# Other rank offsets for the last four batches of an attention and mixer kernel

## The chip, the cores and the metric

The kernel runs on one core of a Trainium2 chip. The metric is the device time of one execution in microseconds; the median of three runs is given. Beside it stands one profiled execution, whose trace the text reads.

## The reference

There are 8 batches of 576 positions, 8 heads of 64. First comes causal attention in a window of 128 positions with a bias that falls with distance, then a mixer: one MLP over the positions (token mixing) and one over the channels, each with a residual.

```python
def attention(q, k, v):                       # (8, 8, 576, 64)
    scores = q @ k.T / 8 + slopes * -abs(rel)  # masked to 0 <= rel < 128
    return softmax(scores) @ v
def mixer(x):                                 # (8, 576, 512)
    h = relu(x.T @ w_tok1) @ w_tok2            # 576 -> 256 -> 576
    u = x + h.T
    return u + relu(u @ w_ch1) @ w_ch2         # 512 -> 1536 -> 512
```

## The kernel before

The kernel works in bf16 with f32 sums. Positions are cut into blocks of 128; two batches make a pair, whose two remainders of 64 positions share one block, TAIL. For each batch `b` there are two strands of work.

`side(b)` is attention and token mixing. For each block the transposed `q` and `k` come from a DMA transpose on SyncE's queue (line 621, into `qkT`). Scores are matmuls of 64 rows (line 672) into both pairs of PSUM banks; ScalarE takes the exponential (695), VectorE masks (705), TensorE multiplies by `v` (739), VectorE normalises into `xb` (752, 755). `token_mix` then multiplies by the token weights (784, 794, ReLU at 802/803, 827, 823 for TAIL), adds the residual into `ub` (845), and SyncE's queue transposes `ub` into `uT` (853).

`main(b)` is channel mixing. `chunk` multiplies `uT` by the first weights (line 1024; all blocks of `uT` must have landed) with a ReLU on ScalarE or VectorE (1030, 1031); `tail_piece` does so for TAIL (1067). The second weights use seven products on halves, as in Strassen's scheme (`second`, line 1212), on sums that VectorE makes (1049); VectorE adds each product to the output (1180), and it is stored (1192). TAIL's second product is at 1112, its sum at 1119, its stores at 1129. The last batch also does its first product in that scheme (`halves`, line 910; `unit`, 946 to 990). Its last product, `last_product`, is at 1241: it adds to a bank after the eviction of product 7, its sums are at 1245 and its two stores at 1248, one from SyncE's queue and one from ScalarE's.

`main(b)` and `side(b+1)` are laid over each other. The order is not written by hand: every step is registered with `plan.op` (engine, estimated cost, rank), and `Plan.run` walks through time with these estimates. Of the steps that an engine could start soonest it takes the one of lowest rank. Ranks within a strand rise by the steps' costs (656 for half a product of 1212, 648 for three matmuls of 1112, 864 for a chunk); `side(b+1)` is squeezed into the first 38% of the ranks of `main(b)`. GpSimd's DMA issues keep the order in which they were registered. Then each step's rank is shifted by a random offset:

```python
        dice = [random.Random(x) for x in SEEDS]
        for o in ops:
            if SEEDS[o.part]:
                o.rank += dice[o.part].uniform(-SHIFT, SHIFT)     # SHIFT = 1500.0
```

The part is set in the loop over the batches, `plan.part = b + 1`, ahead of `main(b)` and `side(b + 1)`. So entry 5 of `SEEDS` covers `main(4)` and `side(5)`, entry 6 `main(5)` and `side(6)`, entry 7 `main(6)` and `side(7)`, entry 8 `main(7)`. An entry of 0 means no offsets; entry 4, for `main(3)` and `side(4)`, is 0 before and after.

Idle instructions are registered last, with a rank above all others: blocks of copies of one column on ScalarE (lines 1286, 1287) and of small memsets on VectorE (1288, 1289), each block after a point of the planned time. Idle matmuls (1296) are put only into gaps of TensorE in the first 60 us of the plan.

Of the kernel before, what the change touches and what calls it, by code (L numbers as in the profile page):

```python
# [10 lines left out]
ACT = mybir.ActivationFunctionType  # L11
# [54 lines left out]
class Plan:  # L66
# [6 lines left out]
    def buf(self, name, choice=None):  # L73
        return Buf(self.rings[name], choice or self.rings[name].each)
# [43 lines left out]
    def run(self):  # L118
        ops = self.ops
# [3 lines that stand above are left out]
                o.rank += dice[o.part].uniform(-SHIFT, SHIFT)  # L123
# [210 lines left out]
RANKH = 0  # L334
RELU = 350
SUMS_AT = 60e3
SEEDS = [45795, 495947, 190309, 331881, 0, 67117, 67408, 179769, 445757]
SHIFT = 1500.0
UNIT_LATE = False
SECOND_LATE = True  # L340
# [28 lines left out]
def kernel(  # L369
# [76 lines left out]
    zero = const.tile([P, P], BF16, name="zero")  # L446
# [25 lines left out]
    pe_, act_, dve_ = nc.tensor, nc.scalar, nc.vector  # L472
# [53 lines left out]
    for i_, name in enumerate("qk"):  # L526
# [3 lines left out]
            out=buf()[:, i, :, :], in_=raw.rearrange("p (h d) -> p h d", h=H)), -100 + i_, makes=buf, after=4.8e3 + 600 * i_)  # L530
# [64 lines left out]
    for e in range(2):  # L595
        def go(e=e):
            for i in range(2):
                dve_.tensor_copy(out=maskt[:, e, :, 0, i * R : (i + 1) * R], in_=masks[:, e, :, 0, 0:R])
            dve_.tensor_copy(out=maskt[:, e, :, 1, :], in_=masks[:, e, :, 1, :])
            dve_.memset(maskt[0:R, e, :, 1, R:P], 0.0)  # L600
# [682 lines left out]
        base += n  # L1283

    for eng, n, cost, at, go in (
            ("ACT", 9, 200, 262e3, lambda: act_.copy(out=zero[:, 0:1], in_=zero[:, 2:3])),
            ("ACT", 9, 200, 262e3, lambda: act_.copy(out=zero[:, 0:1], in_=zero[:, 2:3])),
            ("DVE", 5, 60, 266.5e3, lambda: dve_.memset(zero[:, 1:2], 0.0)),
            ("DVE", 5, 60, 266.5e3, lambda: dve_.memset(zero[:, 1:2], 0.0))):
        plan.op(eng, n * cost, lambda n=n, go=go: [go() for _ in range(n)], 1e9, after=at)  # L1290
# [41 lines left out]
```

## Time and profile before

| | us |
|---|---|
| median of 3 runs | 278.81 |
| lowest, highest | 278.72, 279.33 |
| profiled execution | 278.47 |
| its span, first to last instruction | 276.7 |
| TensorE busy | 268.5 |
| VectorE busy | 209.0 |
| ScalarE busy | 139.2 |

The span leaves out 1.8 us of the execution that lie around the program's instructions. "PE" in a row is TensorE, "PEld" its weight loads, DVE VectorE, ACT ScalarE; SPq and ACTq are the queues from which SyncE and ScalarE issue transfers. `L1212` is line 1212 of the kernel. A timeline row gives start, length, engine, line, operation, output and inputs, and the number of instructions merged; in square brackets stands the engine's idle time just before, with what ended it. The length of a matmul row runs to the end of the last matmul's passage, which overlaps the start of the next row.

### The profile page before, as it was taken

Reading aid. Unit: us, or ns where it says so; the run is one execution under the profiler, and the core shown is the slowest. Engines: PE = TensorE matmul, PEld = TensorE weight load, DVE = VectorE, ACT = ScalarE, POOL = GpSimd, SP = SyncE. Lnnn points to the kernel's source line nnn. Section 1 sums busy time; section 2 is a strip of 40 time slices with the busy share of each in tenths; the row PEclk is TensorE's granted clock in tenths of the full one; section 3 lists DMA queues with packets and bytes.
Section 4 is the critical chain, followed back from the end, with each engine's and each line's share of the span. In section 5 each row is a group of like instructions: output and inputs, shape, how many; then the busy total and the mean of one; then the engine's idle time right before and its main releaser. Section 6 shows DMA issues by size and latency. Waiting matters only on the chain.

```text
span 276.7 us, 6959 instructions
## 1 busy us (share of the span) xinstructions
PE 268.5 (97%) x2789; PEld 179.6 (65%) x2825; DVE 209.0 (76%) x496; ACT 139.2 (50%) x237; POOL 115.8 (42%) x146
## 2 busy tenths in 40 slices
PE   7999999999999999999999999999999999999994
PEld 3665655775686555585567655576667645679884
DVE  7577689978897469853989478763989549886984
ACT  5572884436950298107951096206860079205660
POOL 8998965940356037900585009600472220013000
PEclk9999999999999999999999999999999999999999
DMA  9999999999899999999999979999499750043014
GB/s 132 159 141 164 182 192 189 155 124 207 138 110 111 181 243 133 124 142 181 173 136 151 206 193 100 138 144 243 65 117 97 194 147 2 2 114 135 1 50 143
DMA packets 167553, 38.45 MB, mean 139 GB/s; under 512 B 155808, under 2 KB 166688, under 8 KB 167520
## 3 DMA queue, kind: packets, MB, share of 16 engines
q0 software_dynamic: 116112, 20.03, 94.9%
q1 hardware_dynamic: 50224, 17.57, 33.6%
q10 hardware_dynamic: 1184, 0.39, 0.6%
q8 instruction: 22, 0.36, 0.6%
q14 instruction: 11, 0.09, 0.1%
HBM read 35.85 MB, written 9.44 MB: 164 GB/s over the span
## 4 chain that ended last, share of the span: by engine, by line
PE 89%; DMA 4%; DVE 2%; POOL 1%; ACT 1%; issue 1%; POOLq 0%; ACTq 0%
PE ps L1212 26%; PE ps L1024 22%; PE ps L739 6%; PE ps L672 6%; PE ps L784 5%; PE ps L827 5%; PE ps L1067 4%; PE ps L1112 4%; PE ps L946 3%; DMA WC<-in_moe_w_ch_dram 3%; PE ps L1296 2%; DMA qk<-in_q_dram 2%; PE ps L632 1%; PE ps L794 1%; POOL qk L515 1%
## 5 line engine op out<-in xcount | busy, mean ns | idle before, releaser
L1024 PE MATMUL ps<-uT,WC 128*128 128x512 bf16 x306 | 77.4, 379 | 1.3 <-DMA WC<-in_moe_w_ch_dram 0.3
L695 ACT ACTIVATE pe<-ps 128x1024 bf16<-128x1024 f32 (+1 forms) x76 | 63.4, 888 | 29.9 <-PE ps L672 29.6
L515 POOL DMA_DIRECT2D v<-in_v_dram x40 | 34.1, 866 | 93.6 <-PE ps L739 88.5
L1030 ACT ACTIVATE r<-ps 128x512 bf16<-128x512 f32 x75 | 44.4, 601 | 41.1 <-PE ps L1024 39.1
L1024 PEld LDWEIGHTS <-WC 128*128 128x128 bf16 x328 | 29.1, 98 | 30.6 <-issue 1.4
L705 DVE TENSOR_TENSOR pe<-pe,mask 128x1024 bf16<-128x1024 bf16 (+1 forms) x64 | 38.2, 609 | 8.8 <-ACT pe L695 8.3
L1212 PEld LDWEIGHTS <-r 128*128 128x128 bf16 x372 | 35.9, 98 | 7.2 <-issue 0.2
L515 POOL DMA_DIRECT2D qk<-in_k_dram x39 | 34.5, 891 | 3.0 <-DMA v<-in_v_dram 1.7
L515 POOL DMA_DIRECT2D qk<-in_q_dram x39 | 34.0, 878 | 0.7 <-DMA WC<-in_moe_w_ch_dram 0.6
L1212 PEld LDWEIGHTS <-s 128*128 128x128 bf16 x288 | 27.5, 98 | 6.0 <-issue 1.3
L755 DVE TENSOR_TENSOR xb<-ps,rt 128x256 bf16<-128x256 f32 (+1 forms) x72 | 29.1, 417 | 0.7
L739 PEld LDWEIGHTS <-pe 128*128 128x128 bf16 (+1 forms) x560 | 22.3, 98 | 9.0 <-DVE pe L705 2.6
L739 PE MATMUL ps<-v,pe 128*128 128x65 bf16 (+1 forms) x560 | 26.3, 194 | 0.4 <-DVE pe L705 0.2
L1212 PE MATMUL ps<-WC,r 128*128 128x256 bf16 x192 | 25.4, 273 | 0.0
L1212 PE MATMUL ps<-WT,s 128*128 128x256 bf16 x192 | 24.6, 273 | 0.1
L845 DVE TENSOR_TENSOR ub<-ps,xb 128x512 bf16<-128x512 f32 x34 | 21.2, 683 | 1.8 <-PE ps L827 1.8
L1212 PE MATMUL ps<-WT,r 128*128 128x256 bf16 x180 | 22.4, 273 | 0.0
L672 PEld LDWEIGHTS <-qkT 64*128 64x128 bf16 x560 | 14.8, 94 | 11.2 <-issue 9.8
L1180 DVE TENSOR_TENSOR ob<-ps,ub 128x512 f32<-128x512 f32 x21 | 14.3, 686 | 9.4 <-PE ps L1212 9.2
L672 PE MATMUL ps<-qkT 64*128 64x128 bf16 (+1 forms) x304 | 19.4, 216 | 0.4
L1072 ACT ACTIVATE r2t<-ps 128x512 bf16<-128x512 f32 x12 | 7.2, 603 | 22.7 <-PE ps L1067 22.7
L752 DVE RECIPROCAL rt<-ps 128x4 f32<-128x4 f32 (+1 forms) x76 | 12.5, 175 | 7.6 <-PE ps L739 7.0
(102 smaller groups left out, 347.8 us busy)
## 6 DMA issues: line engine op xcount, KB each, us to landing
v<-in_v_dram POOLq DMA_DIRECT2D x32, 128.0 KB, 5.0
out_dram<-ob SPq DMA_DIRECT2D x16, 256.0 KB, 2.6
qk<-in_k_dram POOLq DMA_DIRECT2D x31, 128.0 KB, 5.1
qk<-in_q_dram POOLq DMA_DIRECT2D x31, 128.0 KB, 5.0
WC<-in_moe_w_ch_dram POOLq DMA_DIRECT2D x8, 384.0 KB, 8.8
out_dram<-raw SPq DMA_DIRECT2D x7, 256.0 KB, 2.7
out_dram<-ob POOLq DMA_DIRECT2D x5, 256.0 KB, 3.6
out_dram<-raw POOLq DMA_DIRECT2D x3, 256.0 KB, 2.9
```

The lines of the kernel that those rows point to most:

```text
L515: nc.gpsimd.dma_start(out=to()[p0 : p0 + n, :, :], in_=rows(src, b, s0, n))
L672: pe_.matmul(wide(e)[:, i, kind, a:z], lhsT=ts[kb]()[e * D : (e + 1) * D, NHP + i, :], rhs=ts[blk]()[e * D : (e + 1) * D, i, a:z], start=n ...
L695: act_.activation(out=pb()[:, e, :, lo:, c0:c1_], in_=wide(e)[:, :, lo:, c0:c1_], func=ACT.Exp, scale=scale)
L705: dve_.tensor_tensor(out=o, in0=o, in1=heads(mk, es), op=ALU.mult)
L739: pe_.matmul(view()[a:z, at, i, :], lhsT=pb()[:, e, i, kind, a:z], rhs=vb()[:, h, 0 : D + 1], start=m == 0, stop=m == len(mms) - 1, skip_g ...
L755: dve_.tensor_tensor(out=x4(), in0=view()[r0:r1_, :, :, 0:D], in1=rt()[r0:r1_, 0:n, :, :].broadcast_to([r1_ - r0, n, 4, D]), op=ALU.mult)
L784: pe_.matmul(t1[j]()[:, :], lhsT=W1[:, c, j * P : (j + 1) * P], rhs=xb()[:, blk, :], start=c == 0, stop=False)
L845: plan.op("DVE", 690, lambda blk=blk, ht=ht, hs=hs: dve_.tensor_tensor(out=ub()[:, blk, :], in0=ht()[:, hs], in1=xb()[:, blk, :], op=ALU.a ...
L1024: pe_.matmul(ct()[:, :], lhsT=WC1[:, cb, t * P : (t + 1) * P], rhs=uT()[:, cb, :], start=cb == 0, stop=cb == NCB - 1)
L1030: plan.op("ACT", 600, lambda t=t, ct=ct: act_.activation(out=r2()[:, t, :], in_=ct()[:, :], func=ACT.Relu), rk, part=(r2, t), uses=[ct], o ...
L1180: dve_.tensor_tensor(out=v, in0=both(bk), in1=src, op=ALU.add)
L1212: pe_.matmul(of(bk, c), lhsT=l(t, c), rhs=w(t), start=first, stop=g == 1 and t == HK - 1, skip_group_check=True)
```

## The change

Four of the nine entries of `SEEDS` are replaced, so the steps of `main(4)` to `main(7)` and of `side(5)` to `side(7)` get other offsets; those of `main(6)` and `side(7)` get none. Each of the two blocks of idle copies on ScalarE has eleven copies where it had nine, with the estimated cost to match (2200 where it was 1800).

```diff
-SEEDS = [45795, 495947, 190309, 331881, 0, 67117, 67408, 179769, 445757]
+SEEDS = [45795, 495947, 190309, 331881, 0, 148233, 244960, 0, 319733]
...
-            ("ACT", 9, 200, 262e3, lambda: act_.copy(out=zero[:, 0:1], in_=zero[:, 2:3])),
-            ("ACT", 9, 200, 262e3, lambda: act_.copy(out=zero[:, 0:1], in_=zero[:, 2:3])),
+            ("ACT", 11, 200, 262e3, lambda: act_.copy(out=zero[:, 0:1], in_=zero[:, 2:3])),
+            ("ACT", 11, 200, 262e3, lambda: act_.copy(out=zero[:, 0:1], in_=zero[:, 2:3])),
             ("DVE", 5, 60, 266.5e3, lambda: dve_.memset(zero[:, 1:2], 0.0)),
             ("DVE", 5, 60, 266.5e3, lambda: dve_.memset(zero[:, 1:2], 0.0))):
```

## Prediction

> **What bounds the kernel now.** I read the page first, for the share of each engine and the transfers of code.
>
> ```profile
> span 276.7 us, 6959 instructions
> ...
> PE 268.5 (97%) x2789; PEld 179.6 (65%) x2825; DVE 209.0 (76%) x496; ACT 139.2 (50%) x237; POOL 115.8 (42%) x146
> ...
> q8 instruction: 22, 0.36, 0.6%
> q14 instruction: 11, 0.09, 0.1%
> ...
> PE 89%; DMA 4%; DVE 2%; POOL 1%; ACT 1%; issue 1%; POOLq 0%; ACTq 0%
> ```
>
> TensorE is busy for 97% of the span, and 89% of the chain that ended last is TensorE. Busy time alone proves little, since matmuls overlap each other, so I looked into the part that the new offsets reach, first at a window of it, then at the starts of its matmuls.
>
> ```profile
> 185.00:221.00 36.00, 35.63 (x378) 24.10 (x382) 25.30 (x56) 16.66 (x24) 11.43 (x14) 1.00 1.07 144
> ```
>
> The columns after the length are the busy time of TensorE, of its weight loads, of VectorE, ScalarE and GpSimd, then the clock, here full (1.00), and DMA. The timeline of TensorE at the start of batch 6 shows the rate:
>
> ```profile
> 215.67 0.81 PE L1112 MATMUL ps<-WC,r2t 128*128 128x512 bf16 x3
> 216.32 1.47 PE L1212 MATMUL ps<-WT,r 128*128 128x256 bf16 x12
> 217.63 1.46 PE L1112 MATMUL ps<-WC,r2t 128*128 128x512 bf16 x6
> 218.92 1.47 PE L1212 MATMUL ps<-WT,r 128*128 128x256 bf16 x12
> 220.45 0.59 PE L1112 MATMUL ps<-WC,r2t 128*128 128x512 bf16 x2
> 221.03 1.02 PE L1024 MATMUL ps<-uT,WC 128*128 128x512 bf16 x4
> 221.99 0.40 PE L672 MATMUL ps<-qkT 64*128 64x128 bf16 x8
> 222.32 1.04 PE L1024 MATMUL ps<-uT,WC 128*128 128x512 bf16 x4
> ```
>
> Take start from start. Three matmuls of 512 columns need 216.32 - 215.67 = 0.65 us, 0.217 each; twelve of 256 columns need 217.63 - 216.32 = 1.31 us, 0.109 each, so one group of six in line 1212 is worth 0.655 us. Every row starts where the row before has used up its matmuls at this rate, with one exception, the start of line 1024 at 221.03. The weight loads show it as well:
>
> ```profile
> 220.12 0.42 PEld L1112 LDWEIGHTS <-r2t 128*128 128x128 bf16 x3
> 221.00 0.56 PEld L1024 LDWEIGHTS <-WC 128*128 128x128 bf16 x4 [0.45 <-issue]
> ```
>
> Three weights were loaded for line 1112, so one matmul record is missing and there were three. The twelve of 218.92 are through at 220.23, the three of line 1112 at 220.88, and line 1024 starts at 221.03: TensorE stood still for 0.15 us. The rows of the transposes that make `uT` say why:
>
> ```profile
> L853 SPq DMA_TRANSPOSE uT<-ub x4: 1217/1229/1288, 213.5 to 217.4; - x4
> ...
> DMA to landing us min/median/max: 2.3/2.7/3.5
> ```
>
> The last of the four is issued at 217.4 and, with the longest landing of 3.5 us, is there at 220.9. Line 1024 reads all four blocks, so it can start only then. What stands between the token mixing and this point, the second products (1212) and the tail block (1112), is cover for that chain, and it was used up to the last group. So the kernel is bound by matmul work, which this change leaves as it is, and by three such handovers plus the end, where order decides whether cover suffices.
>
> **What the change touches, and what each part costs.**
>
> *The matmul work itself: 0.* Ranks decide order alone; every product stays, and the filler matmuls are placed only in the first 60 us of the plan. Order could save or add changes of shape: four matmuls of line 1024 take 221.99 - 221.03 = 0.96 us ahead of line 672 where 4 x 0.217 = 0.87 are due, and the eight of line 672, four pairs of a quarter of 0.217 each, 0.22 us, take 0.33. One excursion to 64 rows costs about 0.2 us. Each score needs both pairs of PSUM banks, so two scores don't stand side by side without waiting for ScalarE; I count the number of excursions as unchanged and keep 0.2 us to either side.
>
> *The handover to batch 5* (new offsets of part 5).
>
> ```profile
> L853 SPq DMA_TRANSPOSE uT<-ub x4: 1190/1252/2225, 176.0 to 182.1; - x4
> ...
> DMA to landing us min/median/max: 2.5/5.0/6.2
> ```
>
> ```profile
> 185.09 1.89 PE L1024 MATMUL ps<-uT,WC 128*128 128x512 bf16 x7
> 186.81 1.47 PE L1212 MATMUL ps<-WT,r 128*128 128x256 bf16 x12
> ```
>
> The last landing is at 182.1 + 2.5 = 184.6 or later, and line 1024 starts at 185.09: at most 0.5 us to spare. But twelve matmuls of line 1212 still stand behind, at 186.81, so another order has 1.31 us of cover in hand here. I cost it at 0, with 0.65 us if one group is missing.
>
> *The handover to batch 6* (part 6). Here nothing is in hand: the margin is -0.15 us and behind 221.03 come only line 1024, which waits for the same transposes, and scores. If the token mixing comes earlier by 0.15 us or one group of the second products later, 0.15 us is gained. If one group of six goes ahead of the token mixing instead, the stall grows by 0.655 us; two groups, 1.31. Offsets of up to 1500 on ranks that lie 656 apart can move a group past two of its neighbours. I take one group, +0.65 us, since the order of before has no spare here, and any other order has more ways to lose cover than to find it.
>
> *The handover to batch 7* (part 7, whose offsets are now all zero).
>
> ```profile
> L946 PE MATMUL ps<-uT,WC x5: 272/272/273, 252.0 to 252.5; 128*128 128x256 bf16 x5
> L853 SPq DMA_TRANSPOSE uT<-ub x4: 1191/1227/1259, 242.6 to 247.8; - x4
> ...
> DMA to landing us min/median/max: 2.3/2.4/3.4
> ```
>
> Landed at 247.8 plus 2.3 to 3.4, 250.1 to 251.2, and needed at 252.0: 0.8 to 1.9 us to spare, so one group may be lost without cost, and two cost at most 0.5. I take 0. SyncE's queue issues these transposes in the planned order too: one that is put behind a transpose for `qkT` (these are issued 1.2 to 1.3 us apart) lands as much later, which is again two groups.
>
> *The end* (part 8).
>
> ```profile
> 270.69 1.15 PE L1112 MATMUL ps<-WC,r2t 128*128 128x256 bf16 x9
> 270.89 0.69 DVE L1180 TENSOR_TENSOR ob<-ps,ob 128x512 f32<-128x512 f32 x1
> 271.67 1.47 PE L1241 MATMUL ps<-WT,r 128*128 128x256 bf16 x12
> 272.36 1.11 SPq L1129 DMA_DIRECT2D out_dram<-raw  x2
> 272.52 0.42 DVE L1245 TENSOR_TENSOR ob<-ps,ub 128x256 f32<-128x256 f32 x1 [0.23 <-PE ps L1241]
> ...
> 273.56 0.54 SPq L1248 DMA_DIRECT2D out_dram<-ob  x1
> 273.64 0.36 ACTq L1248 DMA_DIRECT2D out_dram<-ob  x1
> ```
>
> The last product (1241) adds to a bank that VectorE must have read after the product before: 270.89 to 271.58. Nine matmuls of the tail block, 270.69 to 271.67, fill exactly that wait. If the offsets send them ahead, TensorE idles for up to 0.98 us; three of them, 0.33. Behind the last matmul, the first half's sum is ready at 272.52 + 0.42 = 272.94, but SyncE issues two stores of the tail block until 273.47, so that store goes out at 273.56.
>
> ```profile
> out_dram<-ob SPq DMA_DIRECT2D x3, 128.0 KB, 2.3
> ...
> out_dram<-ob ACTq DMA_DIRECT2D x1, 128.0 KB, 1.8
> ```
>
> It lands at about 273.56 + 2.3 = 275.9, the other half at 273.64 + 1.8 = 275.4; an order that finishes the tail block earlier gains up to 0.4 us here, and pays with the filler. I take 0, from -0.4 to +0.98.
>
> *The four idle instructions.*
>
> ```profile
> 262.75 0.63 ACT L974 ACTIVATE r<-r 128x512 bf16<-128x512 bf16 x1 [2.03 <-DVE r L970]
> ...
> 264.18 2.00 ACT L1286 COPY zero<-zero 128x1 bf16<-128x1 bf16 x9
> 266.21 2.01 ACT L1287 COPY zero<-zero 128x1 bf16<-128x1 bf16 x9
> ```
>
> Nine take 2.00 us, eleven 11/9 of it, 2.45. Two blocks from 264.18 then end at 269.1, and ScalarE's next work is the store at 273.64: 4.6 us are left, cost 0. If a block is placed into a wait like the 2.03 us ahead of 262.75, it delays the ReLU behind it by at most 2.45 us, its whole length. Four instructions also shift where ScalarE's code is loaded. The page has 22 transfers on q8 with 0.36 MB, 16 KB each, and 11 on q14 with 0.09 MB, 8 KB each; no row shows an engine waiting for one, and I cost the shift at 0, bounded by the issue share of the chain, 1% of the span or 2.8 us, all of it over the whole run. The Trainium skill, in Runtime: NRT & Kernel Launch, section Instruction fetch mechanics, says that code comes in blocks of 16 KiB, or 256 instructions, and that crossing into the next is mostly hidden. The 16 KB transfers here agree, the 8 KB ones do not; by that rule the four cost nothing too.
>
> *The sum.* 0 for the work, 0 + 0.65 + 0 for the handovers, 0 for the end and the idle instructions: +0.65 us on the profiled execution, which took 278.47 us (its span of 276.7 and 1.8 around it): 279.1. The median of the runs, 278.81, lies 0.34 above the profiled one, so I expect **279.5 us**, 0.2% more. About 0.2%, 0.56 us, is what a measurement of this kernel can tell from no change, so this forecast lies just beyond it.
>
> **The rivals.**
>
> *Nothing is lost.* The new order covers the handover to batch 6 within a few tenths, as the old one does, and the end keeps its filler. For it: TensorE waits only 0.15 us in the row above, and the unshifted order has a place in this trace too, the handover to batch 4, where line 1024 follows without a gap:
>
> ```profile
> 154.45 1.23 SPq L853 DMA_TRANSPOSE uT<-ub  x1
> ```
>
> ```profile
> 158.30 0.40 PE L672 MATMUL ps<-qkT 64*128 64x128 bf16 x8
> 158.63 1.90 PE L1024 MATMUL ps<-uT,WC 128*128 128x512 bf16 x8
> ```
>
> There 4.2 us lie between the last issue and the use, more than a landing of 3.5. Against it: the cover at batch 6 is used up. Time: 278.3 to 279.3, most likely 278.9.
>
> *Faster.* The gain is bounded: 0.15 at batch 6, 0.4 at the stores, 0.2 for one excursion less, together 0.75 us, 278.06. Since all three are needed to pass 0.56 by much, I give it little. A wider gain would need idle time that the rows above don't leave. The Trainium skill, in Perfetto Trace Analysis, section Identifying the Most-Contended Engine, says that matmul busy time is a poor measure of headroom and that the busy share of weight loads is one to use. By that rule 65% would leave a third of the time free; the trace disagrees, since the starts of line 1212 follow at 0.109 us, the rate above, whatever the share of the loads. I give a gain beyond the bound 2 in 100.
>
> *Two places at once.* The handover to batch 6 loses two groups (1.31) and the end its filler (0.98): +2.3 us, 281.1. Or one block of idle copies falls ahead of a ReLU of the last batch, up to 2.45 us, 281.3. For it: both covers are exactly as long as what they hide. Against it: they are in different parts, with offsets of their own.
>
> *The change does nothing*, because few instructions are ready at a time and the same order comes out. Offsets that span 3000 against steps of 656 make that unlikely; its time is that of the first rival, and it is counted there.
>
> **How the numbers follow.** One group uncovered, at batch 6 or a like loss at the end (0.33 to 1.6 us, 279.1 to 280.4): 0.43, of which 0.07 stays below 0.56. Nothing lost: 0.32. Faster: 0.13, of which 0.02 stays within 0.56 and 0.02 lies beyond the bound. Two places: 0.12. So faster by over 0.2%: 0.11; within: 0.32 + 0.07 + 0.02 = 0.41; slower: 0.36 + 0.12 = 0.48. The range runs from 278.1, the bound of the gain, to 280.9, just below the sum of two places; that leaves out about 0.02 below and 0.1 above. As cases of both signs hold much of it, the likeliest one's own range is 279.1 to 280.4.
>
> **What would show it.** Right: at the start of batch 6 the weight loads of line 1024 show an idle time of 0.8 to 1.2 us instead of 0.45, and its first start follows the last landing of `uT`; batches 5 and 7 start without a gap; the two blocks of copies stand behind the last ReLU and take 2.45 us each. Wrong: line 1024 of batch 6 starts on the heels of line 1112, or the gap is at 1241, where the eviction of line 1180 would be bare, or the last store lands less than 2.3 us behind the last sum. A span that moves by more than these places add up to would mean that something outside them, code loading or the first half, has changed.

## The result and the profile after

| | before | changed |
|---|---|---|
| median, us (11 runs each) | 279.19 | 280.60 |
| lowest, highest | 278.29, 280.33 | 279.82, 281.78 |
| profiled execution | 278.47 | 280.73 |
| its span | 276.7 | 278.9 |

The ratio is 1.0054, with a 95% interval of 1.0035 to 1.0074: the change costs 0.5%, 1.5 us, the interval being 1.0 to 2.1 us. The page of the changed kernel:

```profile
span 278.9 us, 6965 instructions
...
PE 269.2 (97%) x2790; PEld 180.2 (65%) x2825; DVE 209.0 (75%) x497; ACT 139.2 (50%) x237; POOL 116.0 (42%) x146
...
q8 instruction: 22, 0.36, 0.6%
q14 instruction: 11, 0.09, 0.1%
...
PE 82%; DMA 6%; POOL 4%; DVE 4%; issue 2%; ACT 1%; DVEq 0%; POOLq 0%; ACTq 0%
```

The busy times are nearly the same. To place the 2.25 us between the two profiled spans I took three landmarks that both orders share and compared their starts: the first score of the stage in which the orders part (line 672), the first score behind the start of batch 6, and the last product (1241). TensorE's timeline of the changed kernel:

```profile
159.00 0.40 PE L672 MATMUL ps<-qkT 64*128 64x128 bf16 x8
...
219.58 1.47 PE L1212 MATMUL ps<-WT,r 128*128 128x256 bf16 x12
220.89 0.81 PE L1112 MATMUL ps<-WC,r2t 128*128 128x512 bf16 x3
221.53 1.03 PE L1024 MATMUL ps<-uT,WC 128*128 128x512 bf16 x4
222.49 0.40 PE L672 MATMUL ps<-qkT 64*128 64x128 bf16 x8
```

- Up to 159.00, where 158.30 stood before: +0.70. The order there has not changed. The other kernels with this first part reach the point between 158.4 and 159.5, so this is the spread of one execution, and no effect.
- From there to 222.49, where 221.99 stood: 0.20 less. Line 1024 starts at 221.53, right behind the three matmuls of line 1112 (220.89 + 0.65 = 221.54). The wait of 0.15 us at batch 6 is gone. But it was not the old order's: in the four other profiles of that order, taken from runs below, this stretch is 0.15 us shorter (63.54 us for 63.69; 63.49 in the changed kernel), and line 1024 follows the three matmuls of line 1112 at once, as in the run with two memsets (220.35 + 0.65 = 221.00):

```profile
220.35 0.81 PE L1112 MATMUL ps<-WC,r2t 128*128 128x512 bf16 x3
221.00 1.03 PE L1024 MATMUL ps<-uT,WC 128*128 128x512 bf16 x4
```

- From there to 1241, 272.79 for 271.67: +0.62, all of it at the start of batch 7.
- From 1241 to the end: 6.13 for 5.00 us, +1.13.

The start of batch 7, with TensorE's and VectorE's rows of the changed kernel's timeline together:

```profile
246.13 0.68 DVE L1180 TENSOR_TENSOR raw<-ps,raw 128x512 f32<-128x512 f32 x1
...
247.53 0.76 DVE L910 TENSOR_TENSOR tt<-uT 128x512 bf16<-128x512 bf16 x2 [0.73 <-DMA uT<-ub]
248.21 0.68 DVE L1180 TENSOR_TENSOR raw<-ps,raw 128x512 f32<-128x512 f32 x1
...
248.41 0.60 PE L946 MATMUL ps<-uT,WC 128*128 128x256 bf16 x4
...
248.81 0.88 DVE L910 TENSOR_TENSOR tt<-uT,tt 128x512 bf16<-128x512 bf16 x2
...
249.29 0.60 PE L946 MATMUL ps<-uT,WC 128*128 128x256 bf16 x4
249.61 0.68 DVE L1180 TENSOR_TENSOR ob<-ps,ob 128x512 f32<-128x512 f32 x1
...
250.34 1.47 PE L1212 MATMUL ps<-WT,r 128*128 128x256 bf16 x12 [0.46 <-DVE ob L1180]
```

VectorE stands for 0.73 us at line 910, the first step that needs the transposes of batch 7. Behind it in its queue stand two evictions (1180). TensorE has the transposes in time for line 946, but its next twelve matmuls in line 1212 add to a bank that the second eviction must have read, and they start at 250.34. The four of 249.29 were through at 249.73, so TensorE lost 0.6 us to a wait on VectorE, not on the transposes.

Before, VectorE came to line 910 only at 251.04, without any wait for the transposes:

```profile
250.43 0.69 DVE L1180 TENSOR_TENSOR ob<-ps,ub 128x512 f32<-128x512 f32 x1 [1.51 <-PE ps L1212]
251.04 0.75 DVE L910 TENSOR_TENSOR tt<-uT 128x512 bf16<-128x512 bf16 x2
```

In the changed order it is free for line 910 at 246.81 (246.13 + 0.68), 4.2 us earlier, while the transposes, issued from 242.6 to 247.8 before, come only 2.4 to 2.7 us earlier:

```profile
L853 SPq DMA_TRANSPOSE uT<-ub x4: 1191/1220/2242, 240.2 to 245.1; - x4
...
DMA to landing us min/median/max: 2.3/2.9/4.0
```

The end, first the answers on line 1248, the last two stores, before and then after:

```profile
L1248 SPq DMA_DIRECT2D out_dram<-ob x1: 535/535/535, 273.6 to 273.6; - x1
...
DMA to landing us min/median/max: 1.8/1.9/2.1
```

```profile
L1248 SPq DMA_DIRECT2D out_dram<-ob x1: 525/525/525, 274.6 to 274.6; - x1
L1248 ACTq DMA_DIRECT2D out_dram<-ob x1: 361/361/361, 274.8 to 274.8; - x1
...
DMA to landing us min/median/max: 3.2/3.2/3.2
```

Same stores, same size, 1.1 to 1.4 us longer under way. In all profiles of this case the span ends 0.9 to 1.0 us behind the last landing, so a later landing ends the program later by as much. What is new beside them shows in the view of the DMA queues for 0.5 us from 276.4 of the changed kernel:

```profile
DMA packets 7, 0.01 MB, mean 23 GB/s; under 512 B 3, under 2 KB 6, under 8 KB 6
...
q14 instruction: 1, 0.01, 3.9%
q10 hardware_dynamic: 5, 0.00, 3.0%
```

One transfer of code, 8 KB on q14, starts at 276.47, while the last packets of ScalarE's store (q10) trickle in. Before, the last of the eleven lay 0.9 to 1.0 us ahead of those stores; the view from 272.6 to 273.0:

```profile
q1 hardware_dynamic: 142, 0.14, 101.3%
q14 instruction: 1, 0.01, 4.8%
```

The idle copies did what was forecast. From the changed kernel's timeline of ScalarE:

```profile
265.03 0.60 ACT L990 ACTIVATE r<-ps 128x512 bf16<-128x512 f32 x1 [0.87 <-PE ps L946]
...
265.52 2.45 ACT L1286 COPY zero<-zero 128x1 bf16<-128x1 bf16 x11
...
268.01 2.46 ACT L1287 COPY zero<-zero 128x1 bf16<-128x1 bf16 x11
```

### The profile page after: what moved, and what is told of

Read it like the earlier page. It is cut to its first block, busy times and chain, and to the rows that moved or that the text cites. A ratio compares the mean times of both kernels' runs of the same rounds, so it can differ in the third digit from the quotient of the medians.

```text
span 278.9 us, 6965 instructions
## 1 busy us (share of the span) xinstructions
PE 269.2 (97%) x2790; PEld 180.2 (65%) x2825; DVE 209.0 (75%) x497; ACT 139.2 (50%) x237; POOL 116.0 (42%) x146
## 4 chain that ended last, share of the span: by engine, by line
PE 82%; DMA 6%; POOL 4%; DVE 4%; issue 2%; ACT 1%; DVEq 0%; POOLq 0%; ACTq 0%
PE ps L1212 24%; PE ps L1024 23%; PE ps L739 7%; PE ps L672 5%; PE ps L784 5%; PE ps L827 4%; PE ps L1067 4%; PE ps L1112 4%; POOL qk L515 3%; PE ps L946 3%; DMA WC<-in_moe_w_ch_dram 3%; DMA qk<-in_q_dram 2%; PE ps L794 1%; PE ps L1296 1%; DMA uT<-ub 1%
## 5 line engine op out<-in xcount | busy, mean ns | idle before, releaser
L1180 DVE TENSOR_TENSOR ob<-ps,ub 128x512 f32<-128x512 f32 x20 | 13.6, 685 | 8.7 <-PE ps L1212 8.7
```

What stands on the lines that cost most here:

```text
L1180: dve_.tensor_tensor(out=v, in0=both(bk), in1=src, op=ALU.add)
```

## The experiments

The theory after the trace: the order costs something at batch 7, and most of the rest is the code transfer that has moved into the last stores. The open question was whose code it is. The compiled program of the kernel before has 333 instructions for ScalarE and 586 for VectorE, that of the changed one 340 and 582; the traces record four fewer of each, with the same differences. VectorE has one working instruction more (497 for 496 on the pages) and five waits on semaphores fewer (78 for 83 in the traces). The diff names none of this.

**Whose code: copies, memsets.** Nine copies again, with the new offsets:

```diff
-            ("ACT", 11, 200, 262e3, lambda: act_.copy(out=zero[:, 0:1], in_=zero[:, 2:3])),
-            ("ACT", 11, 200, 262e3, lambda: act_.copy(out=zero[:, 0:1], in_=zero[:, 2:3])),
+            ("ACT", 9, 200, 262e3, lambda: act_.copy(out=zero[:, 0:1], in_=zero[:, 2:3])),
+            ("ACT", 9, 200, 262e3, lambda: act_.copy(out=zero[:, 0:1], in_=zero[:, 2:3])),
```

> The new offsets with nine copies in each block, as before the change: TensorE's order is that of the changed kernel row for row. Theory A (a code transfer of 8 KB lies in the last stores and belongs to ScalarE's stream): four instructions fewer move it, the last stores land within 2.3 us again, and only the order is left, about +0.4 us against the kernel before (279.6 for 279.2). Theory B (the transfer belongs to VectorE's or SyncE's stream): nothing moves, +1.5 us, stores landing in 3.2 us. Theory C (the long landing was chance in one profiled execution): its time equals the changed kernel's, +1.5, whatever the last landing of the trace.

Ratio 1.0058 (1.0037 to 1.0079), the last stores landing in 3.2 us, the transfer at 277.5 behind stores of 275.6 and 275.8. The copies change nothing. Theory A is out on this side.

Eleven copies with the old offsets (`9` to `11` in both blocks of the kernel before):

> The offsets of before with eleven copies in each block: TensorE's, VectorE's and SyncE's orders are those of the kernel before. Theory A: the code transfer moves by four instructions of ScalarE; if that puts it into the last stores, +0.8 to +1.1 us, else 0. Theories B and C: 0, within 0.2%.

Ratio 0.9987 (0.9968 to 1.0006), landing in 2.1 us. The four idle instructions cost nothing, alone or together with the offsets.

Seven memsets for five in each of VectorE's idle blocks, in the changed kernel:

```diff
-            ("DVE", 5, 60, 266.5e3, lambda: dve_.memset(zero[:, 1:2], 0.0)),
-            ("DVE", 5, 60, 266.5e3, lambda: dve_.memset(zero[:, 1:2], 0.0))):
+            ("DVE", 7, 60, 266.5e3, lambda: dve_.memset(zero[:, 1:2], 0.0)),
+            ("DVE", 7, 60, 266.5e3, lambda: dve_.memset(zero[:, 1:2], 0.0))):
```

> The changed kernel with seven small memsets where it has five in each of VectorE's two idle blocks, so that VectorE's code is as long as in the kernel before (the changed kernel's is four instructions shorter). Theory B for VectorE: the code transfer goes ahead of the last stores again (before it lay at 272.7, ahead of the store at 273.6), these land within 2.3 us and about +0.4 us is left against the kernel before. Theory A, or B for SyncE, or C: +1.5 us as the changed kernel.

Ratio 1.0034 (1.0018 to 1.0051), and the stores land in 1.9 us, the transfer starting at 274.2 ahead of stores of 275.1 and 275.4. So it is VectorE's. The landing is 1.3 us shorter than in the changed kernel, but only some 0.6 us came back (1.0034 for 1.0054), and the timelines of VectorE and TensorE show where the rest went:

```profile
271.08 0.85 DVE L1288 MEMSET zero<- 128x1 bf16 x7
271.99 0.70 DVE L1289 MEMSET zero<- 128x1 bf16 x6
272.74 0.69 DVE L1180 TENSOR_TENSOR ob<-ps,ob 128x512 f32<-128x512 f32 x1
```

```profile
271.87 1.15 PE L1112 MATMUL ps<-WC,r2t 128*128 128x256 bf16 x9
273.48 0.71 PE L1241 MATMUL ps<-WT,r 128*128 128x256 bf16 x5 [0.46 <-DVE ob L1180]
```

The longer blocks push back the eviction ahead of the last product, and TensorE waits 0.6 us for it, which is the bare eviction that the prediction named, for another reason.

**The transfer by itself.** The cleanest test keeps every order and takes away four instructions of VectorE from the kernel before (`5` to `3` memsets in both blocks):

> The kernel before, offsets and copies included, with three small memsets where it has five in each of VectorE's two idle blocks: every engine's order stays, only VectorE's code is four instructions shorter, as long as the changed kernel's (582 for 586). Theory B, VectorE's code transfer in the last stores: the transfer moves from 1 us ahead of the last store to behind its issue, that store lands in 3.2 us instead of 2.1, and the time rises by 1.1 us (0.4%) with no order changed. Rival, the long landing belongs to the changed order of stores: 0, within 0.2%, landing in 2.1 us.

Ratio 1.0042 (1.0028 to 1.0056): 1.2 us, from four idle instructions fewer. The answer on line 1248 and the view of the queues from 275.8 to 276.3:

```profile
L1248 SPq DMA_DIRECT2D out_dram<-ob x1: 535/535/535, 274.3 to 274.3; - x1
L1248 ACTq DMA_DIRECT2D out_dram<-ob x1: 358/358/358, 274.4 to 274.4; - x1
...
DMA to landing us min/median/max: 3.0/3.1/3.3
```

```profile
q1 hardware_dynamic: 92, 0.08, 46.0%
q14 instruction: 1, 0.01, 6.3%
```

One memset fewer again in each block (`5` to `2`; one per block, not the two that the text below names) should carry the transfer past the landing:

> The kernel before with two small memsets where it has five in each of VectorE's idle blocks, two per block less than in the run with three: VectorE's code has 580 instructions for 586, all orders stay. Theory: what costs is a code transfer that starts between the last stores' issue and their landing; with 580 it starts only after they have landed, as in the run without the transpose wait (580, transfer at 278.8, landing in 2.1 us). So 0 within 0.2%, landing in 2.1 us. Rival: shorter code always costs, +1.1 us or more.

Ratio 0.9999 (0.9982 to 1.0016), the transfer at 277.3, after the end of the span, and line 1248 as before:

```profile
L1248 SPq DMA_DIRECT2D out_dram<-ob x1: 536/536/536, 273.5 to 273.5; - x1
...
DMA to landing us min/median/max: 1.8/2.0/2.1
```

So it is not length that costs but the place: between issue and landing of the last stores.

**The order's share.** Two ways of taking the transfer out of the changed kernel. First, as long a code as before, with the memsets away from the end:

```diff
-            plan.op("DVE", 395, lambda: dve_.tensor_copy(out=xt()[far, :], in_=xb()[own, TAIL, :]), rank(0),
+            plan.op("DVE", 395, lambda: (dve_.tensor_copy(out=xt()[far, :], in_=xb()[own, TAIL, :]), b >= 4 and dve_.memset(zero[:, 1:2], 0.0)), rank(0),
```

> The changed kernel with four small memsets more on VectorE, one behind each copy at line 779 of batches 4 to 7, so that its code is as long as before the change (586) and nothing is added at the end; all other orders are the changed kernel's. Theory B: the last stores land in about 1.9 us, and TensorE's last product is not held up as it was where the memsets stood in the idle blocks; 1.2 us less than the changed kernel, +0.3 us against the kernel before, which is the order's own share. Rival: +1.5 us as the changed kernel.

Ratio 1.0011 (0.9991 to 1.0031), landing in 2.2 us. Second, a shorter code (`5` to `3` memsets in both blocks of the changed kernel):

> The changed kernel with three memsets for five in each of VectorE's idle blocks: 578 instructions for 582, nothing added and no order changed. Theory: the transfer starts after the last stores have landed, these land in 2.1 us, +0.3 to +0.6 us against the kernel before, the order's share. Rival, only as long a code as before helps: +1.5 us as the changed kernel.

Ratio 1.0033 (1.0011 to 1.0056), the transfer at 279.4, behind the end, and line 1248:

```profile
L1248 ACTq DMA_DIRECT2D out_dram<-ob x1: 358/358/358, 274.9 to 274.9; - x1
...
DMA to landing us min/median/max: 1.8/2.0/2.2
```

They took 0.4 and 0.2 of the 0.54% away; the order is left with 0.1 to 0.3% (0.3 to 0.9 us, intervals from below zero to 0.56%). It varies by execution: VectorE starts line 910 at 0.09 us behind the last landing that it needs, wherever that falls, in each profile in which it waits there. In this order TensorE's wait at batch 7 was 0.2 us in the profile of the first of these two, 0.8 in that of the second and 1.0 in that with nine copies. That last profile also shows a wait at the start of batch 5, which the changed kernel's own does not:

```profile
186.00 1.06 PE L1067 MATMUL ps<-uTt,WC 128*128 128x128 bf16 x16
187.33 1.04 PE L1024 MATMUL ps<-uT,WC 128*128 128x512 bf16 x4 [0.28 <-DMA uT<-ub]
```

The sixteen were through at 186.90, so 0.4 us were lost.

**The wait at batch 7.** All four of VectorE's differences at line 910 read a weight tile, which is there long before:

```diff
-        for i, p, n, need in ((1, lambda: uT()[:, x, hi], lambda: uT()[:, x, lo], []),
+        for i, p, n, need in ((1, lambda: WC1[:, x, hi], lambda: WC1[:, x, lo], []),
...
```

> The changed kernel, but the four differences of line 910 are made from a weight tile instead of uT, so the batch's first product is not the reference's; VectorE no longer waits there for the transposes of batch 7, and its code is two wait instructions shorter (580). My theory of the stall: VectorE's wait of 0.7 us for uT and TensorE's 0.6 us in line 1212 behind it are both gone, 0.6 us less than the changed kernel if the last stores stay as slow (+0.9 us against before). Rival: the eviction at line 1180 is late for another reason, for instance more VectorE work ahead of it, and TensorE's gap stays at 0.6 us.

Ratio 1.0021 (1.0004 to 1.0038). TensorE's wait is gone, as its and VectorE's rows show:

```profile
247.56 0.75 DVE L910 TENSOR_TENSOR tt<-WC 128x512 bf16<-128x512 bf16 x2
...
249.62 0.68 DVE L1180 TENSOR_TENSOR ob<-ps,ob 128x512 f32<-128x512 f32 x1
...
250.13 0.60 PE L946 MATMUL ps<-uT,WC 128*128 128x256 bf16 x4
...
250.56 1.47 PE L1212 MATMUL ps<-WT,r 128*128 128x256 bf16 x12
```

250.13 + 0.44 = 250.57: line 1212 follows at once. The median lies 0.2% above the kernel before, where I expected 0.9 us: with 580 instructions the transfer also left the last stores (278.8, against a landing of 277.1 at the latest), so what I had expected of the tail was wrong. In exchange this run lost 0.4 us at the start of batch 5.

Both edits, four memsets and line 910:

> Both edits at once, the four memsets at line 779 and line 910 reading a weight tile (part of the first product of the last batch is not the reference's); VectorE's code has 584 instructions. If the stall of batch 7 and the code transfer are the whole difference, this is no slower than the kernel before: -0.3 to +0.2 us. If something else in the order costs time, +0.5 us or more.

Ratio 1.0049 (1.0036 to 1.0062): a miss. With 584 instructions the transfer started at 275.0, 0.8 us behind the issue of a store, and the stores took 2.7 us. That is some 0.5 us of the 1.4; its profile shows no place for the rest. Eight memsets instead of four put the transfer at 270.6:

> As the run with both edits, but with eight memsets at line 779 instead of four, so that VectorE's code has 587 instructions for 584 and the transfer lies ahead of the last stores (line 910 again reads a weight tile). Theory: the +0.5% of that run was the transfer, which with 584 still began 0.8 us after the issue of a store; now -0.2 to +0.4 us against the kernel before. Rival: the order costs more than the profiles show, +1 us or more again.

Ratio 1.0007 (0.9987 to 1.0027), landing in 2.1 us. This is 1.2 us less than with four, of which the landings explain 0.6; the other half stays open. Without the transfer in the stores and without the wait of line 910, the changed order takes as long as the old one within what can be told. The profiles say the same of the stretch from the first score (159.00 in the changed kernel) to line 1241: 113.2 to 113.4 us in five with the old order, 113.4 to 114.6 in four with the changed order, 113.3 in these last two.

**Parts 5 and 6 alone.** `SEEDS = [45795, 495947, 190309, 331881, 0, 148233, 244960, 179769, 445757]`:

> The changed kernel with the old offsets for parts 7 and 8, so that only the offsets of parts 5 and 6 are new (eleven copies). My theory of the order: batch 6 starts without its wait of 0.15 us (gain 0.2 as in the changed kernel) and the stall of 0.62 us at the start of batch 7, which lies in part 7, is gone: -0.2 us, plus up to 1.1 for the last stores if the code transfer falls into them. Rival: the stall at batch 7 follows from the offsets of parts 5 and 6, then +0.4 or more.

Ratio 1.0118 (1.0094 to 1.0142), 3.3 us: the rival's direction, and far more. The profile has no stall of one kind but a string of them, 0.6 us at the start of batch 5 and some 3 us in all from 256 us on, the longest 1.0 and 0.9 in lines 1212 and 1241. The tail has little part in it: the code transfer starts 1.0 and 0.4 us behind the issue of the two last stores, which land in 2.5 and 2.1 us. The offsets of later parts work only on top of the order that the earlier ones left; I did not take this order apart further.

**A better version?** The changed order offers none. The kernel before has one weak place that the prediction named, the store held behind SyncE's:

```diff
-                (nc.sync, nc.scalar)[c].dma_start(out=out[b, HS + c * P : HS + (c + 1) * P, 0:HN], in_=ob()[:, 0:HN])
+                nc.scalar.dma_start(out=out[b, HS + c * P : HS + (c + 1) * P, 0:HN], in_=ob()[:, 0:HN])
```

> The kernel before with both stores of the last product issued from ScalarE's queue, so that the first is not held behind two stores of the tail block on SyncE's queue. Theory: the last landing comes about 0.3 us earlier, 0.1% faster, at the edge of what the runs can tell; the trace shows the first store going out at the end of its sum instead of 0.6 us later. Rival: the two stores share one queue and the second lands later, 0 or slower.

Ratio 0.9992 (0.9975 to 1.0009). The first store went out at 273.69, and the last landed at 276.1, 3.7 us behind the start of line 1241 (272.37) where it was 4.0 before. The gain is of the size expected and cannot be told from none.

## Why the prediction was right, and where it was not

The direction, slower, was right, and 280.6 lies in the range. The likeliest time, 279.5, was 0.65 us above its reference; the measured difference was 1.5. The steps fared worse than the number: the one loss in the sum did not occur, and the two that did were put at 0. That 280.6 lies in the range is therefore luck, helped by a range that took in both signs.

- *The matmul work: 0.* Right. TensorE was busy for 269.2 us against 268.5, and the landmarks account for the span without it.
- *The handover to batch 6: +0.65.* Wrong, and it was the whole of the sum. The new order covers it: 0.2 us were gained against the profile above, 0.05 against the other four of the old order. The margin of -0.15 us was that of one execution, and I read it as the order's, and as a place that can only get worse. The token mixing came earlier in the new order, its first transposes issued at 211.6 where they were at 213.5, with the landmark ahead of them 0.7 later.
- *The handover to batch 7: 0, with 0.8 to 1.9 us to spare.* Wrong: 0.6 us in the profile, 0.2 to 1.0 in others of this order. The margin was taken from the old order, where the product starts at 252.0; in the new one it starts at 248.4, 3.6 us earlier, and the transposes only 2.4 to 2.7. And I looked at TensorE's use of `uT`, not at VectorE's, which came first and held up evictions in its queue.
- *The handover to batch 5: 0, up to 0.65.* Within its bounds: 0 to 0.4 us in profiles of this order, 0.6 with the offsets of parts 5 and 6 alone.
- *The end's filler: 0.* Right for TensorE in the changed kernel: nine matmuls of line 1112 still cover the eviction, within 0.1 us.
- *The idle instructions and the code: 0, bounded by 2.8 us.* The copies cost nothing, as said. The bound held in size, though it was drawn from idle time of the engines and the cost came as a later landing. The value was the step that failed most: 1.2 us, most of the result. The prediction tied the shift to ScalarE's four instructions; it came from four that VectorE lost, five waits fewer against one working instruction more. The Trainium skill, in Runtime: NRT & Kernel Launch, section Instruction fetch mechanics, calls the cost of crossing into the next block mostly hidden. No row above has an engine waiting for code, which agrees; the last transfer still cost 1.2 us, by way of the stores. The sign that I named for something outside the listed places, a span that moves by more than they add up to, is what led there.
- *The rivals.* "Two places at once" was nearest: two places, though neither as described.

## What to carry to other kernels

When an order changes, the number of instructions on an engine can change with it (586 to 582 here), and so the place of code transfers. Look at the last transfer of code against the last store, because a store that lands later there ends the program later; a few idle instructions more or fewer move the transfer. Margins of a handover are read from the order in which they were measured and don't carry over to another, and a margin of a tenth of a us not even to another execution; of all engines that wait for the transfer, the one to check is the first in time, and what stands behind it in its queue.

## What the runs showed of the hardware

The time of a store of 128 KB depends on what else is in flight to a degree that I had not expected. The last two land in 1.7 to 2.2 us when the 8 KB of code start ahead of their issue, at most 0.1 us behind it, or after they have landed, and in 3.0 to 3.3 us when the code starts 1.5 to 1.9 us behind their issue (582 instructions, three kernels). Between the two lie 2.1 and 2.5 us for 0.4 and 1.0 us behind (parts 5 and 6 alone), and 2.7 us for 0.6 to 0.8 (both edits). From the start of line 1241 to the end of the span it is 6.12 to 6.13 us in those three kernels, and 4.97 to 5.04 in the seven that have the transfer away from the stores and the last product and its stores unchanged and on time.

The transfer itself takes 0.31 us (276.47 to 276.78 in the changed kernel), and why it adds 1.1 us to a landing is open. The packets of the trace show a part of it. ScalarE's last store has sixteen packets of 4 bytes. In the run with the memsets at line 779, which has the same order, all of them have ended 1.69 us behind the issue, and the landing is seen 0.5 us later. In the changed kernel fifteen have ended by then too, but one ends at 276.92, 0.5 us behind the others, and the landing is seen at 277.99, 1.1 us later. One such packet, 0.3 to 0.7 us behind the other fifteen, is there in all five profiles in which the transfer starts 0.4 to 1.9 us behind this store's issue; in the others with one store on that queue the last is at most 0.04 us behind. So in the changed kernel one packet held up accounts for about half, and the rest lies between the last packet and the landing; what holds up either, no run shows.
